# Moving a query projection and a pair of score rounds in the prologue of a two-cache decode kernel

## Chip, cores, metric

One core of one Trainium2 chip. The metric is device microseconds (us) of one execution; each quoted time is the median of the runs named with it. In the profile the engines are called PE (TensorE), DVE (VectorE), ACT (ScalarE), POOL (GpSimd) and SP (SyncE).

## The reference, cut to what matters

Two single-token attention blocks, A and B, with 32 query heads of 128 each. A reads all 32,768 keys and values of 32 heads (the large cache, 268 MB each). B reads the last 4,096 keys and values of 8 heads, each serving four query heads (the small cache, 8 MB each).

```python
q = (x @ wq).reshape(B, Sq, H, Dh)                  # query projection
scores = einsum("bhqd,bhkd->bhqk", q, k) * Dh**-0.5
p = softmax(scores)
o = einsum("bhqk,bhkd->bhqd", p, v)
out = o.reshape(B, Sq, H * Dh) @ wo                 # then A and B side by side
```

## The kernel before

All large loads are 4 MiB and go through one DMA queue (issued by SP) in program order. There are four big buffers: two for keys, two for values. The value buffers first hold the two query weights: B's in `v[0]`, A's in `v[1]`. A "unit" is one key buffer: TensorE (PE) transposes it in 16 batches of eight, VectorE (DVE) copies each batch out, and PE multiplies by the queries, one "pair" of steps behind. A "round" then takes the maximum, exponentiates, transposes the probabilities (`psPT`) and multiplies them with the values (`PV`). A "gather" is a small matmul at the end of a round. B has two rounds of one unit each, in the prologue; A has 32 rounds of two units, in a loop on PE.

```python
self.load_wq("B")                      # -> v[0]
for g in range(2):
    self.load_kv("k", "B", g, 0, 0)    # -> k[0], k[1]
self.load_wq("A")                      # -> v[1]
self.emit_qproj("B")
for g in range(2):
    self.emit_unit("B", g, 0, 0)       # transposes and scores of k[g]
    self.emit_round_end("B", g, 0)     # maximum, exponential, psPT
    if g == 0:
        self.emit_qproj("A")           # reads v[1]
    self.load_kv("v", "B", g, 0, 0)    # -> v[g], when its query weight has been read
    self.emit_PV("B", g, 0, 0)
    self.emit_gather("B", g, 0)
self.emit_spread("B")
# then the loop over A: per round, loads k[0], k[1], units, round end, loads v[0], v[1], PVs, gather
```

In this kernel each instruction raises at most one semaphore (a counter on which another engine waits), for one listener. If PE's instruction already has a listener (`to="dve"`), the message for SP is carried by PE's *next* instruction without one:

```python
# in emit_qproj: DVE is the listener, so SP must wait for a later PE instruction
o = self.op("pe", mm, (self.xsem[name], 16), self.landed("v", slot), self.accread, to="dve")
self.free["v"][slot] = o
# in assign()
if to is None:
    to = next((c for c in users + pending), None)
pending = [c for c in dict.fromkeys(pending + users) if c != to]
```

The units' transposes, `PV` and the second half of a gather all have a listener. The first score operation of a pair and the first half of a gather have none, so they carry SP's messages.

## Time and profile before

| | before |
|---|---|
| time, 3 runs | 1341.73 us (1341.38 to 1341.76) |
| profiled span | 1340.3 us |
| read from memory | 570.43 MB, mean 426 GB/s |
| PE / DVE / ACT busy | 71% / 59% / 5% |

From the page of the kernel before: the mean busy share of the 16 DMA engines (in tenths) and the GB/s they moved, in 40 equal slices of 33.5 us, and the main queue (packets, MB, share of the engines' span).

```profile
DMA  9799999999999999999999999999999999999998
GB/s 397 303 437 428 433 428 434 431 432 432 427 436 428 434 432 428 435 429 434 429 432 433 430 434 429 433 432 429 435 429 432 433 429 433 431 432 430 431 434 353
...
q1 hardware_dynamic: 21700, 570.44, 99.1%
```

Between the first slice and the last, the stream is full but for the second slice: at 303 GB/s, about 10 us of loading are missing there, (432 - 303)/432 of 33.5 us. From 140 to 1300 us the trace has a mean of 432 GB/s at a DMA share of 1.00, and no slice has more than 437. That a load could not go faster is not shown; with the DMA engines busy throughout, I took it that what a change to the prologue can win is a hole in this stream.

The stretches around it (window in us and its length; busy time of PE, PE's weight loads, DVE, ACT and POOL; granted TensorE clock; DMA share; GB/s):

```profile
51.00:52.00 1.00, 0.00 (x0) 0.00 (x0) 0.00 (x0) 0.00 (x0) 0.00 (x0) 0.50 0.91 377
52.00:53.00 1.00, 0.00 (x0) 0.00 (x0) 0.00 (x0) 0.00 (x0) 0.00 (x0) 0.50 0.22 90
53.00:54.00 1.00, 0.00 (x0) 0.00 (x0) 0.00 (x0) 0.00 (x0) 0.00 (x0) 0.50 0.06 25
54.00:60.00 6.00, 4.36 (x38) 1.37 (x39) 1.40 (x4) 0.00 (x0) 0.00 (x0) 0.50 0.00 0
60.00:61.00 1.00, 1.00 (x11) 1.00 (x12) 0.02 (x1) 0.00 (x0) 0.00 (x0) 0.50 0.65 98
61.00:62.00 1.00, 1.00 (x12) 1.00 (x10) 0.84 (x2) 0.00 (x0) 0.00 (x0) 0.50 0.54 213
62.00:63.00 1.00, 1.00 (x13) 1.00 (x11) 0.84 (x2) 0.00 (x0) 0.00 (x0) 0.50 1.00 410
```

DMA all but stops at 52.3 us and is back at full rate at 62. What SP and PE do meanwhile, from the timeline (start, length, engine, line; in brackets, idle time before it and what ended that):

```profile
30.70 29.20 SPq L291 DMA_DIRECT2D vbuf<-in_B_v_cache_dram  x2
...
44.24 3.55 PE L422 MATMUL psACC<-x_A,vbuf 128*128 128x1 bf16 x128 [2.58 <-DMA vbuf<-in_A_wq_dram]
...
54.03 3.59 PE L553 MATMUL psACC<-vbuf,ptsb 128*16 128x512 bf16 x32 [6.23 <-DMA vbuf<-in_B_v_cache_dram]
...
59.23 0.74 PE L596 MATMUL psG<-oc_B,hsel_B 128*32 128x1 f32 x4 [1.61 <-DVE oc_B L582]
...
59.94 10.77 SPq L291 DMA_DIRECT2D kbuf<-in_A_k_cache_dram  x2
```

A merged line with `x2` runs from the start of its first issue to the end of its last: the first of B's value loads was issued at 30.70, the second ended its issue at 59.90. It goes into the buffer that the second query projection had finished reading at 47.8, but SP heard of it from the gather at 59.23. The two key loads of A stand behind it. The DMA queue's own waits up to 140 us (total us, times, longest) say the same: one wait of 28.4 us ended by a gather.

```profile
SPq L291 <- PE psS L486: 65.1, 5, 21.6
SPq L291 <- PE psG L596: 57.0, 3, 28.4
```

### The profile page before, as it was taken

How to read it: one execution, taken by the hardware profiler on the slowest of the kernel's cores; microseconds unless marked ns; L12 is line 12 of the kernel's file. 1: busy time of each engine (PE TensorE's matmuls, PEld its weight loads, DVE VectorE, ACT ScalarE, POOL GpSimd, SP SyncE). 2: the span in 40 equal slices, each digit the busy share in tenths (PEclk: the TensorE clock that was granted, in tenths of full speed). 3: DMA queues.
4: the chain of work that ended last, by engine and by line, in shares of the span. 5: the costliest groups of instructions: out<-in, count | busy, mean ns of one | idle time of the engine just before them, and what ended most of it. 6: DMA issues, size and time to landing. Idle time of an engine off the chain costs nothing.

```text
span 1340.3 us, 41412 instructions
## 1 busy us (share of the span) xinstructions
PE 958.2 (71%) x19416; PEld 773.7 (58%) x19416; DVE 791.7 (59%) x1662; ACT 61.2 (5%) x201; POOL 2.0 (0%) x15
## 2 busy tenths in 40 slices
PE   3577767777666777766777686666877766777776
PEld 3455656566555665655556565555656655565663
DVE  3365656665555666555566665555676555566652
ACT  0000000000000000000000000000000000000000
POOL 0000000000000000000000000000000000000000
PEclk9677888898788889887888888788889787888888
DMA  9799999999999999999999999999999999999998
GB/s 397 303 437 428 433 428 434 431 432 432 427 436 428 434 432 428 435 429 434 429 432 433 430 434 429 433 432 429 435 429 432 433 429 433 431 432 430 431 434 353
DMA packets 22003, 570.64 MB, mean 426 GB/s; under 512 B 2530, under 2 KB 2532, under 8 KB 2788
## 3 DMA queue, kind: packets, MB, share of 16 engines
q1 hardware_dynamic: 21700, 570.44, 99.1%
q8 instruction: 10, 0.16, 0.1%
q10 hardware_dynamic: 288, 0.00, 0.0%
q14 instruction: 5, 0.04, 0.0%
HBM read 570.43 MB, written 0.00 MB: 426 GB/s over the span
## 4 chain that ended last, share of the span: by engine, by line
DMA 64%; PE 26%; issue 0%; DVE 0%; SPq 0%
DMA kbuf<-in_A_k_cache_dram 62%; PE psT L463 22%; PE psS L486 4%; DMA kbuf<-in_A_wo_dram 2%; PE psPT L625 0%; DVE out_sb L629 0%; SPq L291 0%
## 5 line engine op out<-in xcount | busy, mean ns | idle before, releaser
L466 DVE COPY kt<-psT 128x1024 bf16<-128x1024 bf16 x1056 | 655.7, 684 | 211.1 <-PE psT L463 208.9
L463 PE MATMUL psT<-ident,kbuf 128*128 128x128 bf16 x8448 | 576.5, 234 | 135.7 <-DMA kbuf<-in_A_k_cache_dram 126.1
L463 PEld LDWEIGHTS psT<-ident,kbuf 128*128 128x128 bf16 x8448 | 537.1, 106 | 227.7 <-DMA kbuf<-in_A_k_cache_dram 134.0
L553 PE MATMUL psACC<-vbuf,ptsb 128*2 128x128 bf16 (+1 forms) x8256 | 190.5, 273 | 45.4 <-ACT ptsb L531 22.0
L553 PEld LDWEIGHTS psACC<-vbuf,ptsb 128*2 128x2 bf16 (+1 forms) x8256 | 170.5, 106 | 66.7 <-ACT ptsb L531 30.5
L486 PE MATMUL psS<-kt,qw 128*32 128x512 bf16 x2048 | 157.6, 385 | 15.2 <-DVE kt L466 15.2
L528 PE MATMUL psPT<-ident,psb 128*128 128x128 bf16 x136 | 20.7, 307 | 139.3 <-ACT psb L518 139.3
L582 DVE SCALAR_TENSOR_TENSOR oc_A<-psACC,hot_A,oc_A 128x128 f32<-128x128 f32 x48 | 16.9, 351 | 146.2 <-PE psACC L553 146.2
L528 PEld LDWEIGHTS psPT<-ident,psb 128*128 128x128 bf16 x136 | 11.7, 130 | 149.4 <-ACT psb L518 149.4
L518 ACT ACTIVATE psb<-psS,nb_A 128x512 bf16<-128x512 f32 x32 | 22.0, 687 | 1164.5 <-DVE nb_A L517 1164.5
L486 PEld LDWEIGHTS psS<-kt,qw 128*32 128x32 bf16 x2048 | 34.0, 95 | 57.7 <-DVE kt L466 31.0
L579 DVE TENSOR_SCALAR oc_A<-psACC,hot_A 128x128 f32<-128x128 f32 x16 | 5.6, 351 | 92.8 <-PE psACC L553 92.8
L504 DVE TENSOR_REDUCE tr_in<-psS 128x1 f32<-128x512 f32 x34 | 23.5, 692 | 17.3 <-PE psS L486 17.3
L596 PE MATMUL psG<-oc_A,hw 128*32 128x128 f32 (+1 forms) x128 | 14.1, 220 | 22.1 <-DVE oc_A L582 19.4
L507 DVE COPY m<-tr_a 1x16 f32<-1x16 f32 (+1 forms) x136 | 22.3, 164 | 2.6
L513 DVE COPY b_A<-mr_A 1x16 f32<-1x16 f32 x128 | 21.1, 165 | 2.4
L596 PEld LDWEIGHTS psG<-oc_A,hw 128*32 128x32 f32 x128 | 6.5, 109 | 27.3 <-issue 27.3
L531 ACT ACTIVATE ptsb<-psPT 128x512 bf16<-128x512 bf16 x34 | 20.3, 597 | 17.6 <-PE psPT L528 17.6
L565 DVE TENSOR_SCALAR oc_A<-oc_A,alpha_A 128x129 f32<-128x129 f32 x16 | 4.6, 289 | 16.5 <-ACT alpha_A L521 16.5
L422 PE MATMUL psACC<-x_B,vbuf 128*128 128x1 bf16 x128 | 3.6, 165 | 13.3 <-DMA vbuf<-in_B_wq_dram 13.3
L422 PEld LDWEIGHTS psACC<-x_B,vbuf 128*128 128x128 bf16 x128 | 3.5, 104 | 13.3 <-issue 13.3
L521 ACT ACTIVATE alpha_A<-cm_A,nb_A 128x1 f32<-128x1 f32 x32 | 9.0, 282 | 0.0
(71 smaller groups left out, 106.3 us busy)
## 6 DMA issues: line engine op xcount, KB each, us to landing
kbuf<-in_A_k_cache_dram SPq DMA_DIRECT2D x64, 4096.0 KB, 28.1
vbuf<-in_A_v_cache_dram SPq DMA_DIRECT2D x64, 4096.0 KB, 28.3
kbuf<-in_B_k_cache_dram SPq DMA_DIRECT2D x2, 4096.0 KB, 27.9
vbuf<-in_B_v_cache_dram SPq DMA_DIRECT2D x2, 4096.0 KB, 18.3
vbuf<-in_B_wq_dram SPq DMA_DIRECT2D x1, 4096.0 KB, 12.4
vbuf<-in_A_wq_dram SPq DMA_DIRECT2D x1, 4096.0 KB, 41.8
kbuf<-in_B_wo_dram SPq DMA_DIRECT2D x2, 2048.0 KB, 25.6
kbuf<-in_A_wo_dram SPq DMA_DIRECT2D x1, 1536.0 KB, 22.2
```

The costliest lines, as they stand in the source:

```text
L463: inst = e.transpose(T[:, 128 * k:128 * k + 128], src[:, DH * tile:DH * tile + DH], self.ident[:, :])
L466: self.copies.append(self.op("dve", lambda v: v.tensor_copy(KT[:, :], T[:, :]), o, to="pe"))
L486: inst = e.matmul(self.S[32 * c:32 * c + 32, :], lhsT=win, rhs=self.kt[(bb + c // 2) % NKT][:, 512 * (c % 2):512 * (c % 2) + 512], start=f ...
L504: o = dve(lambda v: v.reduce_max(tr["in"][:, 0:1], self.S[:, :], axis=AXX), self.sdone, self.k_pool)
L507: x = dve(lambda v, c=c: v.tensor_copy(m4[0:1, W * c:W * c + W], tr["a"][32 * c:32 * c + 1, 0:W]), o)
L513: x = dve(lambda v, c=c: v.tensor_copy(t["b"][32 * c:32 * c + 1, 0:W].rearrange("p (k h) -> p k h", k=KC), t["mr"][0:1, k, :].unsqueeze(1) ...
L518: self.sread = self.op("act", lambda s: s.activation(out=self.psb[:, :], in_=self.S[:, :], func=ACTF.Exp, bias=t["nb"][:, k:k + 1], scale= ...
L528: inst = e.transpose(PT[:, 128 * jj:128 * jj + 128], self.psb[:, 128 * jj:128 * jj + 128], self.ident[:, :])
L531: self.ptread = self.op("act", lambda s: s.activation(out=self.ptsb[:, :], in_=PT[:, 0:512], func=ACTF.Copy), self.psread, to="pe")
L553: inst = e.matmul(acc[32 * c:32 * c + HG, 0:w], lhsT=pt[:, col:col + HG], rhs=vv[:, :, 16 * kc + 4 * c + jj, :], start=(kc == 0 and jj == ...
L582: self.oop = dve(lambda v, src=src, hot=hot: v.scalar_tensor_tensor(out=oc, in0=src, scalar=hot, in1=oc, op0=ALU.mult, op1=ALU.add), pv, b ...
L596: self.gath = self.op("pe", lambda e, c=c, c2=c2: e.matmul(self.G[0:32, c0 + c:c0 + c2], lhsT=win, rhs=t["oc"][:, c:c2], start=False, stop ...
```

## The change

Its intent: take both of B's score rounds before any of B's values, and do A's query projection inside the second unit, so that the buffer is released earlier. The round's end is split in two for that: statistics (`emit_stats`) and probability transpose (`emit_PT`). No computing is added or removed; what is cut from the diff below is bookkeeping (the rescaling factor is kept per round).

```diff
         self.load_wq("A")
         self.emit_qproj("B")
+        self.emit_unit("B", 0, 0, 0)
+        self.emit_stats("B", 0, 0)
+        self.emit_PT("B", 0, 0)
+        self.emit_unit("B", 1, 0, 0, lambda: self.emit_qproj("A"))
+        self.emit_stats("B", 1, 0)
         for g in range(2):
-            self.emit_unit("B", g, 0, 0)
-            self.emit_round_end("B", g, 0)
-            if g == 0:
-                self.emit_qproj("A")
+            if g == 1:
+                self.emit_PT("B", g, 0)
             self.load_kv("v", "B", g, 0, 0)
             self.emit_PV("B", g, 0, 0)
             self.emit_gather("B", g, 0)
@@
-    def emit_unit(self, name, g, r, u):
+    def emit_unit(self, name, g, r, u, late=None):
         slot = u if name == "A" else g
         for pr in range(4):
             for st in (2 * pr, 2 * pr + 1):
                 for half in range(2):
                     self.emit_T(slot, st, half)
+            if pr == 3 and late:
+                late()
             self.pending.append((name, g, r, u, pr, self.nbatch - 4))
             if len(self.pending) > 1:
                 self.emit_S(self.pending.pop(0))
```

More of the change, by code (lines that the diff above doesn't have):

```diff
@@ L337, in plan @@
         self.gath = self.lop = self.qcopy = self.hcopy = None
+        self.alpha = {}
         self.constants()
@@ L362, in plan @@
                 self.emit_unit("A", g, r, u)
-            self.emit_round_end("A", g, r)
+            self.emit_stats("A", g, r)
+            self.emit_PT("A", g, r)
             for u in range(2):
@@ L493, in emit_S, with emit_stats @@
         self.sdone = o
-    def emit_round_end(self, name, g, r):
+    def emit_stats(self, name, g, r):
         self.emit_S(self.pending.pop(0))
@@ L520, in emit_round_end, with emit_PT @@
             accum_out=t["rs"][:, k:k + 1]), o, self.psread, to="pe")
-        self.alpha = self.op("act", lambda s: s.activation(
+        self.alpha[name, k] = self.op("act", lambda s: s.activation(
             out=t["alpha"][:, k:k + 1], in_=t["cm"][1 - k if r else k][:, 0:1], func=ACTF.Exp,
             bias=t["nb"][:, k:k + 1], scale=self.SCALE), o, to="dve")
+    def emit_PT(self, name, g, r):
+        d, t = self.X[name], self.c[name]
         PT = self.PT[:, :].bitcast(BF16)
@@ L535, in emit_round_end @@
             self.hcopy = self.op("act", lambda s: s.activation(
-                out=self.hw[:, :], in_=t["hsel"][:, 32 - HG * g:64 - HG * g], func=ACTF.Copy, scale=on),
+                out=self.hw[:, :], in_=t["hsel"][:, 32 - d["HG"] * g:64 - d["HG"] * g], func=ACTF.Copy, scale=on),
                 self.k_sel, to="pe")
@@ L565, in emit_PV @@
             first = dve(lambda v: v.tensor_scalar_mul(t["oc"][:, :], t["oc"][:, :], t["alpha"][:, k:k + 1]),
-                        self.alpha, self.oop, self.gath, to="dve")
+                        self.alpha[name, k], self.oop, self.gath, to="dve")
         def denominator():
             if r > 0:
-                return dve(lambda v: v.tensor_add(lcol, lcol, t["rs"][:, k:k + 1]), first, self.alpha, to="dve")
-            return dve(lambda v: v.tensor_copy(lcol, t["rs"][:, k:k + 1]), self.alpha, first, to="dve")
+                return dve(lambda v: v.tensor_add(lcol, lcol, t["rs"][:, k:k + 1]), first, self.alpha[name, k], to="dve")
+            return dve(lambda v: v.tensor_copy(lcol, t["rs"][:, k:k + 1]), self.alpha[name, k], first, to="dve")
         if d["units"] == 1:
```

## The prediction

> **What bounds the kernel.** DMA. The page's DMA row is full in nearly all of the 40 slices: 570.4 MB read at a mean of 426 GB/s, and 20 us windows from 60 to 1320 us show a DMA share of 0.98 to 1.02 at 416 to 439 GB/s. [...] PE is busy 71%, DVE 59%. Each 4 MiB load takes about 9.7 us at that rate. The only hole outside start and tail is in the third slice (303 GB/s): 1 us windows show the share at 0.22 in 52-53, 0.06 in 53-54, zero from 54 to 60, full again from about 61: some 8.3 us.
>
> **Why the hole.** The first five loads (both query weights, two small-cache key tiles, first value tile) end at about 52.3 us. The sixth, the second value tile, goes to the buffer of the second query weight, so it needs that query projection (PE 44.2 to 47.8). Its release is signalled only by PE's next operation without an assigned listener, the gather after the first values (59.23): the queue's waits name that gather, and the timeline shows the issue at about 59.5. The first large-cache loads stand behind it in queue order.
>
> **What the change does.** No computing is added or removed. After the first round's probabilities PE goes straight on with the second unit's transposes, then the query projection, then the scores, whose first operation now carries the release.
>
> Costs from the trace:
> - First probability transpose ends at 41.7, unchanged.
> - Second unit's transposes: from first to last 10.6 us in unit one (24.5 to 35.1), 10.0 in unit two (59.9 to 69.9). They start cold: TensorE clock 0.50 from 40 us. [...] End at about 52.2.
> - Query projection: 3.55 us cold; warm perhaps 2.0 to 2.3 (estimate from the value product, which took 3.58 cold and 1.96 to 2.30 warm). End 54.2 to 55.8.
> - First score operation to issue: 0.40 us (69.93 to about 70.33 before).
>
> So the sixth load is issued at 54.6 to 56.2 instead of 59.5: 3.3 to 4.9 us earlier. The next two large-key loads follow at once, as both key buffers are free by then. The next value load waits for the first values' gather, at about 62, and the one after for the second's, about 72, while three queued loads keep DMA busy until about 85: no new hole. All of the gain is on the critical path, because the loop is DMA bound and a shift of its start goes through to the end. The hole is halved, not closed: some 4 us stay.
>
> **Prediction.** 1341.7 - 4.1 = 1337.6 us, range 1335.5 to 1340.0. Faster by over 2%: 0.005; within 2%: 0.99; slower by over 2%: 0.005.
>
> **What would show it right.** Hole from about 52.3 to 56.5 us in 1 us windows; second value load released by a score operation, not a gather; second query projection at about 52 us; loop's DMA share still about 1.00; everything later about 4 us earlier. Wrong: a second hole before 110 us, or one that stays 8 us.
>
> **What would make it wrong.** The transposes run cold longer (later issue); a release signalled by another operation than I think; DMA resuming later than 1.1 us after issue; or the shift given back in the loop's first iterations.

Its sum: transposes to 52.2, projection to 54.2 to 55.8, issue at 54.6 to 56.2 instead of 59.5, so 3.3 to 4.9 us, 4.1 in the middle, and 1341.7 - 4.1 = 1337.6 us. "At that rate" means about 431 GB/s, the mean from 60 to 1320 us in the trace of the kernel before; the same trace has eight transposes in 0.85 us at a recorded clock of 0.50 (60 to 62 us).

## The result, and the profile after

| | before | after |
|---|---|---|
| time | 1341.74 us, 4 runs (1341.38 to 1342.23) | 1338.36 us, 4 runs (1336.93 to 1339.06) |
| ratio after / before | | 0.9973 (95% interval 0.9956 to 0.9990) |
| profiled span | 1340.3 us | 1335.2 us |

A ratio here is the mean time of one kernel's fast runs over that of the other's of the same rounds, so it is not quite the ratio of the medians. The change is small, 0.27%, and clear of the noise.

The same two rows of the page, for the changed kernel: the second slice went from 303 to 377 GB/s, and no other slice moved by more than 10 GB/s.

```profile
DMA  9999999999999999999999999999999999999998
GB/s 394 377 427 436 426 436 426 438 425 438 426 437 427 436 428 434 430 434 429 435 429 435 428 435 429 435 429 434 430 432 432 432 432 431 432 432 432 431 433 354
```

The same stretches for the changed kernel. The hole starts at the same time and ends some 5 us sooner.

```profile
51.00:52.00 1.00, 1.00 (x46) 1.00 (x43) 1.00 (x3) 0.00 (x0) 0.00 (x0) 1.00 0.83 344
52.00:53.00 1.00, 1.00 (x46) 1.00 (x43) 0.23 (x1) 0.00 (x0) 0.00 (x0) 1.00 0.32 123
53.00:54.00 1.00, 1.00 (x46) 1.00 (x43) 0.00 (x0) 0.00 (x0) 0.00 (x0) 1.00 0.08 33
54.00:55.00 1.00, 1.00 (x21) 0.52 (x21) 0.19 (x1) 0.00 (x0) 0.00 (x0) 0.76 0.00 0
55.00:56.00 1.00, 1.00 (x16) 0.40 (x12) 0.24 (x1) 0.00 (x0) 0.00 (x0) 0.50 0.56 66
56.00:57.00 1.00, 1.00 (x16) 0.39 (x12) 0.90 (x4) 0.00 (x0) 0.00 (x0) 0.50 0.56 213
57.00:58.00 1.00, 1.00 (x13) 0.31 (x8) 0.91 (x5) 0.00 (x0) 0.00 (x0) 0.53 1.04 442
```

The timeline of the changed kernel, second unit to first gather:

```profile
40.71 5.45 PE L470 MATMUL psT<-ident,kbuf 128*128 128x128 bf16 x64
...
50.87 3.34 PE L427 MATMUL psACC<-x_A,vbuf 128*128 128x1 bf16 x128
...
54.14 1.57 PE L493 MATMUL psS<-kt,qz 128*32 128x512 bf16 x16
...
54.59 0.37 SPq L291 DMA_DIRECT2D vbuf<-in_B_v_cache_dram  x1
...
55.00 0.98 SPq L291 DMA_DIRECT2D kbuf<-in_A_k_cache_dram  x2
...
60.59 0.47 PE L606 MATMUL psG<-oc_B,hsel_B 128*32 128x1 f32 x4 [1.99 <-DVE oc_B L592]
```

PE starts the second unit's transposes at 40.71, with no wait for values; the projection follows at 50.87; the score operation at 54.14 tells SP, which issues the second value load at 54.59 and both key loads of A right behind it. In the queue's waits, time moved from the gathers to the score operations:

```profile
SPq L291 <- PE psS L493: 90.0, 6, 24.4
SPq L291 <- PE psG L606: 36.0, 3, 18.7
```

The profiled run was the fastest of its four, so 5.1 us of difference between the spans is more than the 3.4 us between the medians. The spread itself is taken up below.

### The profile page after: what moved, and what is told of

It is laid out like the page before. It is cut to its first block, busy times and chain, and to the rows that moved or that the text cites. A ratio compares the mean times of both kernels' runs of the same rounds, so it can differ in the third digit from the quotient of the medians.

```text
span 1335.2 us, 41413 instructions
## 1 busy us (share of the span) xinstructions
PE 954.6 (71%) x19416; PEld 771.0 (58%) x19416; DVE 791.1 (59%) x1662; ACT 61.1 (5%) x201; POOL 2.0 (0%) x15
## 4 chain that ended last, share of the span: by engine, by line
DMA 64%; PE 26%; issue 0%; DVE 0%; SPq 0%
DMA kbuf<-in_A_k_cache_dram 63%; PE psT L470 22%; PE psS L493 4%; DMA kbuf<-in_A_wo_dram 2%; PE psPT L635 0%; DVE out_sb L639 0%; SPq L291 0%
## 5 line engine op out<-in xcount | busy, mean ns | idle before, releaser
L563 PEld LDWEIGHTS psACC<-vbuf,ptsb 128*2 128x2 bf16 (+1 forms) x8256 | 169.0, 106 | 67.1 <-ACT ptsb L541 30.5
L538 PEld LDWEIGHTS psPT<-ident,psb 128*128 128x128 bf16 x136 | 11.6, 130 | 145.0 <-ACT psb L525 144.8
```

Of the source, the lines that this page charges most:

```text
L538: inst = e.transpose(PT[:, 128 * jj:128 * jj + 128], self.psb[:, 128 * jj:128 * jj + 128], self.ident[:, :])
L563: inst = e.matmul(acc[32 * c:32 * c + HG, 0:w], lhsT=pt[:, col:col + HG], rhs=vv[:, :, 16 * kc + 4 * c + jj, :], start=(kc == 0 and jj == ...
```

## The experiments

Every kernel gave a correct result. "Hole" below is the loading that is missing: the sum over 1 us windows of (432 - GB/s)/432, once for 50 to 65 us and once for 115 to 135 us. (It counts the slow ramp at 60 to 62 us as well, so it gives 9.3 us for the kernel before, where the prediction read 8.3 from the shares.) "Issue" is when SP issues B's second value load.

| kernel | issue | hole at 50-65 | hole at 115-135 | span of the profiled run | median, 5 runs (lowest, highest) | ratio to before |
|---|---|---|---|---|---|---|
| before | 59.5 | 9.3 | 0.2 | 1340.3 | 1342.18, 9 runs (1341.85, 1342.51) | 1 |
| after, again | 55.2 | 4.9 | 0 | 1335.7 | 1339.01 (1337.44, 1339.18) | 0.9976 |
| e1 signal only | 48.2 | 0 | 4.7 | 1336.8 | 1339.57 (1338.51, 1340.18) | 0.9981 |
| e2 key load first | 59.5 | 0.2 | 4.0 | 1335.7 | 1337.58 (1337.48, 1338.93) | 0.9969 |
| e4 late release | 61.5 | 11.1 | 0.5 | 1342.1 | 1343.86 (1343.70, 1345.86) | 1.0019 |
| e3 projection early | 50.9 | 0.3 | 0 | 1332.3 | 1335.53 (1334.07, 1336.62) | 0.9952 |
| e5 projection first | 54.5 | 4.1 | 0.5 | 1335.0 | 1336.62 (1335.88, 1337.06) | 0.9958 |
| e6 key load first, on changed | 55.3 | 0.2 | 1.9 | 1333.3 | 1335.59 (1335.01, 1336.90) | 0.9954 |
| e7 two signals | 48.1 | 0 | 0 | 1332.6 | 1334.74 (1334.30, 1335.34) | 0.9946 |
| e8 early with signal | 49.0 | 0 | 0 | 1332.8 | 1334.57 (1334.22, 1334.68) | 0.9943 |
| e9 early and loop signal | 47.9 | 0 | 0 | 1332.6 | 1334.32 (1334.20, 1334.78) | 0.9942 |
| after, third time | 57.0 | 6.8 | 0.2 | 1337.7 | 1338.36 (1337.45, 1339.45) | 0.9971 |

The runs of before are those of the first batch; in the other two batches its median was 1342.18 and 1342.16. The three batches ran on three different chips; each ratio is to the kernel before in the same batch. Issue, hole and span of before are those of its profile above.

### e1: the release alone, in the old order

Theory A was that the time is the hole, and the hole is the late release of one buffer. Rival B was that the gain comes from PE's order of work, which lets PE reach the loop earlier.

```diff
                 self.emit_qproj("A")
+                self.op("pe", lambda e: e.transpose(
+                    self.T[0][:, :].bitcast(BF16)[:, 0:128], self.ident[:, :], self.ident[:, :]))
```

> The kernel before, with its order of work kept; one small transpose into an idle PSUM bank follows the second query projection and carries the release of its buffer to the DMA queue. Theory A (the time is the hole in the DMA stream, and the hole is the late release of that buffer): the second value load is issued at about 48 us instead of 59.5, the hole of about 8.3 us closes, and the kernel takes about 1333.5 us, less than the changed kernel. Theory B (the gain comes from the order of PE's work, which lets the loop start earlier): nothing in PE's order has moved, so about 1341.7 us.

The first part came true: SP heard from the small transpose, issue was at 48.2 us, and the hole was gone. But the time was 1339.57, not 1333.5. Windows of this kernel (same columns) show where the gain went:

```profile
52.00:61.00 9.00, 5.09 (x59) 2.43 (x59) 1.99 (x5) 0.00 (x0) 0.00 (x0) 0.70 1.01 422
121.00:125.00 4.00, 0.98 (x5) 0.37 (x5) 0.35 (x1) 0.00 (x0) 0.00 (x0) 0.66 0.03 8
```

A new hole of some 4 us had opened at 121 us. SP's issues around it:

```profile
31.31 17.23 SPq L291 DMA_DIRECT2D vbuf<-in_B_v_cache_dram  x2
...
95.03 10.08 SPq L291 DMA_DIRECT2D kbuf<-in_A_k_cache_dram  x2
124.14 0.80 SPq L291 DMA_DIRECT2D vbuf<-in_A_v_cache_dram  x2
```

The last loads before it are the two keys at 95.03 to 105.11; the next is the first value load of the loop's second round, at 124.14, told by the gather of the first round (123.87). Closing the first hole moved the stream forward by 8 us or so, but PE's chain to that gather did not move, and it had only some 5 us to spare: in the kernel before the seven loads after the hole would have lasted from 61 to about 129 us (7 times 9.7), and the gather came at 123.6. Part of e1's chain are two stalls of PE, 1.51 and 3.95 us, that no wait in the trace explains (see the last section). Without them the gather would have come at about 118.4 us (an estimate: 123.87 less both), before DMA ran dry at about 121. No run takes the stalls away, so how much of the second hole is theirs stays open. Theory A alone had fallen, and so had B alone, since time was won without a change of order.

### e2: queue order alone

```diff
             self.load_kv("v", "B", g, 0, 0)
+            if g == 0:
+                self.load_kv("k", "A", 0, 0, 0)
@@
-                self.load_kv("k", "A", g, r, u)
+                if i > 0 or u > 0:
+                    self.load_kv("k", "A", g, r, u)
```

> The kernel before, with PE's order and every release kept; only the first large-cache key load goes into the DMA queue ahead of the second small-cache value load instead of behind it. Theory A: it is issued at about 35.5 us and follows the fifth load without a gap, while the value load is still issued at about 59.5, so the hole closes and the time is about 1333.5 us. Theory B: about 1341.7 us.

The key load filled the first hole though the value load was issued as late as before (59.5 us, with a hole of 0.2 us and not 9.3), which shows that it was the head of the queue that blocked. The time was 1337.58, again 4 us short of the expectation, with the same new hole at 121 us (4.0 us).

### e4: the changed order with the old release

The comment is added here, and a second part of the edit, which keeps that operation in `gath0`, is cut.

```diff
             if g == 1:
                 self.emit_PT("B", g, 0)
+                self.free["v"][1] = self.gath0   # the first gather's first half
```

> The changed kernel with PE's order kept, but the second value load is made to wait for the gather of the first values again, as in the kernel before. Theory A: the load is issued at about 60.9 us, some 1.3 us later than in the kernel before, and the time is about 1343 us; the whole gain is gone. Theory B: PE's order is that of the changed kernel, so about 1338 us.

Theory A was right here: 1343.86 us, slower than the kernel before. SP's issues:

```profile
30.61 31.23 SPq L291 DMA_DIRECT2D vbuf<-in_B_v_cache_dram  x2
61.88 0.98 SPq L291 DMA_DIRECT2D kbuf<-in_A_k_cache_dram  x2
```

The second value load's issue ended at 61.84, 1.9 us later than before, and the median is 1.7 us higher. So PE's order wins nothing by itself while the release is late. Together, e1 and e4 suggested a theory A2: there are two limits, the release of the weight's buffer and, behind it, PE's chain up to the first values of the loop. The change moves both.

### after again

> The changed kernel itself, on the same chip as the others. Both theories: about 1338.4 us, with a spread over its runs of about 2 us as in the first four; the second value load is issued at about 54.6 to 55.4 us and a hole of about 3.5 us stays in the DMA stream.

1339.01 us and a spread of 1.7 us, about as expected; the hole was 4.9 us and not 3.5.

### e3: the projection two pairs earlier

```diff
-            if pr == 3 and late:
+            if pr == 1 and late:
```

> The changed kernel with one number changed: the second query projection follows the second pair of steps of the second unit, not the fourth. The last batch showed that in the kernel before an early release alone only moves the hole: a new one of some 4 us opens at 121 us, as the first values of the loop are released at 124 us by a PE chain that starts late. Theory A2 (two limits: the release of the query weight's buffer, and the PE chain up to the first values of the loop; the change moves both): the second value load is issued at about 50 us, before the queue runs dry at 52, the first hole closes, the loop's first gather comes at about 113 us, well before the queue runs dry at about 121, and the time is about 1334.0 us (8.2 us below before). Theory A (one hole, one release): the same here. Rival C (some 4 us of any such gain are always lost to something not yet seen): about 1338 us, no better than the changed kernel.

Both holes were gone, and rival C was out: 1335.53 us, 3.5 us below the changed kernel in the batch before, though 1.5 above the expectation. The load was issued at 50.9 us, only 1.4 before the queue ran dry, and the runs spread over 2.6 us.

### e5: the projection in front of the unit

```diff
-        self.emit_unit("B", 1, 0, 0, lambda: self.emit_qproj("A"))
+        self.emit_qproj("A")
+        self.emit_unit("B", 1, 0, 0)
```

> The changed kernel with the second query projection taken out of the second unit and put right before it, so only the order of scores ahead of values is left of the change. PE then waits for that weight, which lands at about 44 us, and the release comes with the first score operation after the projection and 64 transposes. Theory A2: issue at about 53.4 us, against about 55 in the changed kernel, a hole of some 2 us, and about 1.2 us less than the changed kernel: some 1337.3 us, so the place within the unit is not what wins. Theory D (the place within the unit is what wins, since PE no longer waits for the weight): slower than the changed kernel by the wait of 2.6 us, about 1341 us.

1336.62 us: theory D fell, and the place *within* the unit is not what the change wins by. The issue came at 54.5 us (53.4 expected), so the hole was 4.1 us and not 2. PE did wait 2.5 us for the weight, and it cost nothing, since the release came no later.

### e6: queue order, on the changed kernel

The edit is that of e2, made to the changed kernel.

> The changed kernel with the first large-cache key load ahead of the second small-cache value load in the DMA queue, the same edit that took the kernel before to about 1337.6 us with a new hole at 121 us. Theory A2: the first hole closes; the second values now land only at about 73 us, PE waits for them, the loop's first transposes start at about 78 us and its first gather comes at about 118 us, just before the queue runs dry at about 121, so no second hole, or one below 1 us: about 1334.5 us. Theory A: 1334. Rival C: 1338.

1335.59 us, 2.0 below e2. The second hole shrank from 4.0 to 1.9 us, not to under 1: PE had to wait until 73.95 us for B's second values, which now stood behind a key load, so the loop's first transposes began at 81.9 and not at 78, and its first gather at 120.9. I had allowed 5 us from those values to the loop; the second product, gather and spread took 8. The second limit works as A2 says, with less slack than I had counted.

### e7: two signals, no change of order

e1, and in the loop:

```diff
                 self.emit_PV("A", g, r, u)
+                if u == 0:
+                    self.op("pe", lambda e: e.transpose(
+                        self.T[0][:, :].bitcast(BF16)[:, 0:128], self.ident[:, :], self.ident[:, :]))
```

> The kernel before with the early release of the first of these experiments, and a second small transpose in the loop, after the first value product of each round, which carries the release of that value buffer instead of the gather after the second product. PE's order of work is that of the kernel before. Theory A2: the loop's first value buffer is released at about 117 us instead of 124, the second hole closes as well, and the time is about 1334 us, though PE reaches the loop as late as before. Theory B (PE must reach the loop earlier): the hole at 121 us stays and the time is about 1339.5 us.

1334.74 us, 7.4 us below before and well below the changed kernel, with PE's order of work untouched. The windows in which e1 had its hole:

```profile
52.00:61.00 9.00, 5.20 (x58) 2.42 (x59) 1.96 (x5) 0.00 (x0) 0.00 (x0) 0.69 1.01 421
121.00:125.00 4.00, 0.98 (x6) 0.37 (x6) 0.35 (x1) 0.00 (x0) 0.00 (x0) 0.69 1.00 426
```

PE is as busy from 121 to 125 us as in e1, 0.98 us, and stalls as long just before its last two matmuls (3.96 us), but DMA moved 426 GB/s there and not 8: SP issued the first of the loop's value loads at 116.93 us and not at 124.14. So it was not PE's late arrival as such, but the gather that carried the message for a buffer that had been read some 7 us earlier. That is the clearest of these runs: both holes closed when nothing was changed but who says that a buffer is free, and when.

### e8, e9 and the spread of the changed kernel

The kernel before spread over 0.7 us in nine runs, the changed one over about 2 us. In e8 the projection comes after the first pair, followed by a small transpose that carries the release, so that nothing is close to a limit. e9 adds e7's loop signal.

```diff
-        self.emit_unit("B", 1, 0, 0, lambda: self.emit_qproj("A"))
+        self.emit_unit("B", 1, 0, 0, lambda: self.emit_qproj("A") or self.signal())
@@
-            if pr == 3 and late:
+            if pr == 0 and late:
@@
+    def signal(self):
+        self.op("pe", lambda e: e.transpose(
+            self.PT[:, :].bitcast(BF16)[:, 512:640], self.ident[:, :], self.ident[:, :]), self.ptread)
```

> The changed kernel with the second query projection after the first pair of steps of the second unit, and a small transpose right behind it that carries the release. The earlier run that closed the first hole with the changed order issued its load at 50.9 us, only 1.4 us before the queue runs dry, and its runs spread over 2.6 us. Theory E (kernels whose hole is ended by an instruction behind clock-dependent transposes spread; one with slack everywhere doesn't): issue at about 48.2 us, no hole, about 1334.3 us and a spread of 1 us or less. Rival (the spread comes from elsewhere, say from the last projections): about 1335.5 us with a spread of 2 us or more.

> The run before in this batch with the early release of the loop's first value buffer as well. Theory A2: with no hole left after the start, a further early release is worth nothing: the same within 0.5 us, about 1334.3 us. If it is faster by 1 us or more, some hole in the loop is still open.

> The changed kernel again, on the same chip as these two, for a direct comparison: about 1338.8 us, spread about 2 us, and a hole of about 3.5 to 4 us in its profile. The two above should be about 4.5 us below it.

e8 took 1334.57 us with a spread of 0.46 us, e9 1334.32, the changed kernel beside them 1338.36 with a spread of 2.0. (Its profile, of its slowest run, has a hole of 6.8 us where 3.5 to 4 were expected.) Windows of e8 in both places:

```profile
52.00:61.00 9.00, 8.52 (x132) 5.02 (x129) 7.30 (x16) 0.00 (x0) 0.00 (x0) 0.92 1.01 421
121.00:125.00 4.00, 4.00 (x73) 3.22 (x70) 4.00 (x8) 0.00 (x0) 0.00 (x0) 1.00 1.03 442
```

The third profile of the changed kernel happened to be of a slow run (1339.45 us), the first of a fast one (1336.93), so the two can be laid side by side. PE up to the operation that tells SP, first the fast run of the changed kernel, then the slow one:

```profile
24.39 5.08 PE L470 MATMUL psT<-ident,kbuf 128*128 128x128 bf16 x64 [7.59 <-DMA kbuf<-in_B_k_cache_dram]
...
40.71 5.45 PE L470 MATMUL psT<-ident,kbuf 128*128 128x128 bf16 x64
...
50.87 3.34 PE L427 MATMUL psACC<-x_A,vbuf 128*128 128x1 bf16 x128
54.14 1.57 PE L493 MATMUL psS<-kt,qz 128*32 128x512 bf16 x16
```

```profile
24.53 6.60 PE L470 MATMUL psT<-ident,kbuf 128*128 128x128 bf16 x64 [7.83 <-DMA kbuf<-in_B_k_cache_dram]
...
42.27 6.30 PE L470 MATMUL psT<-ident,kbuf 128*128 128x128 bf16 x64
...
53.28 3.34 PE L427 MATMUL psACC<-x_A,vbuf 128*128 128x1 bf16 x128
56.55 1.05 PE L493 MATMUL psS<-kt,qz 128*32 128x512 bf16 x16
```

The first unit's 64 transposes took 5.08 us in the one and 6.60 in the other, the second unit's 5.45 and 6.30: 2.37 us together. The issue was 2.39 us later (54.59 and 56.98), the span 2.5 us longer. The second profile of the changed kernel lies between the two (5.29 and 5.58 us, issue at 55.2, span 1335.7). The transposes start at a slower pace, eight in 0.85 us (12 or 13 of them in a 1 us window), and reach their full pace, 32 in 1.96 us, at different times. In the second unit the recorded clock goes from 0.50 to 1.00 at about 44.3 us in the fast run and 47.6 in the slow one, 3.6 and 5.3 us after the unit's first transpose. In the first unit the clock column reads 1.00 throughout, and only the pace shows the change, at about 27 and 30.5 us. So the change of pace came at different distances from the start of the work; what sets the distance is not shown. In the kernel before, the end of the hole depends on a load that landed at 54.0 and not on the transposes, so it does not spread; and e8, which has slack, does not either. The tie between clock and spread rests on these three profiles and on e8; why e5's runs lie below the changed kernel's, with like profiles (1335.0 and 1335.2), was not tried. One reason is at hand: in e5 only one of the two stretches of transposes counts, because the landing of the weight at 44.4 hides the other.

## Why the prediction was right, point by point

- **What bounds the kernel.** Right. All thirteen profiles have 431 to 432 GB/s from 140 to 1300 us, and the span follows the sum of the holes to within 2.6 us, over a range of 11.6. (From kernels with the old hole to those without any, 9.5 counted us of hole gave 7.6 us of span. Most of the rest is lost at the end: the page's last slice has 353 GB/s in the kernel before and 339, 332 and 337 in e7, e8 and e9, which is 1.1 to 1.6 us of loading.)
- **Why the hole.** Right, and shown by three independent edits: an earlier message (e1), another load at the head of the queue (e2), and the old message put back (e4).
- **Issue between 54.6 and 56.2 us.** Measured 54.6, 55.2 and 57.0 in three profiles, the last outside the range. The terms: the second transposes gave way to the projection at 50.9 in the first profile (predicted 52.2), 51.5 and 53.3 in the others; the projection took 3.34 us in all three. So in the first two profiles an early warm-up made good a projection that was longer than hoped, and that is luck. The hope of 2.0 to 2.3 us for a warm projection was wrong. It was taken from a product with 128 columns moving per matmul, while here one column moves, and 3.34 us over 128 is 26.1 ns each. The projection hardly gained from the clock: 27.7 ns each at a recorded clock of 0.50 (3.55 us, in the kernel before), 26.1 at 1.00. (Each of these matmuls also loads its own weights, and the weight loads keep the same pace, 3.31 us for 128; no run here tells which of the two sets the pace.)
- **The whole gain goes through to the end.** Right for this change: no second hole, and 5.1 us of span for 4.9 us of earlier issue in the first profile. The reason given, a DMA-bound loop, was not enough: e1 and e2 have the same loop, and each lost some 4 us again at 121 us. The prediction followed the loads only to 85 us. That the change also moved the loop's first gather, from 123.57 to 117.35 us, was not worked out in it as a condition, so this point was in part luck.
- **1337.6 us.** Measured 1338.36; 1339.01 and 1338.36 in later batches, all inside the range of 1335.5 to 1340.0. The gain was 3.2 to 3.8 us by medians and not 4.1. The mis-sized term is probably the projection: 3.34 us, where the middle of the predicted 2.0 to 3.55 is 2.8; the transposes' end scattered around the predicted 52.2 (50.9, 51.5, 53.3).
- **What it did not see.** That the old order had only some 5 us of slack at the loop's first values. The prediction did not count this place for either kernel, and so theory A expected 1333.5 of e1 and e2. A gain of 8 us was never there for the early release alone.

## What to carry to other kernels

When a DMA-bound kernel has a hole in its stream, ask first which instruction *tells* the queue that the buffer is free, and not only which one frees it: here the two were 11 us apart, and one tiny instruction that carries the message (twice) won 7.4 us, twice as much as the changed order of work (3.2 to 3.8). After closing a hole, look for the next place where the stream has little slack, because the gain can stop there (in e1 and e2 some 4 us of it were lost again at 121 us); and if a kernel's runs spread more than before, look whether its limit now sits behind work whose pace changes with the clock (here the second unit's 64 transposes took 5.45 us in a fast run, with the clock at 1.00 from about 44.3, and 6.30 in a slow one, from about 47.6).

The fastest kernels here are e8 and e9: 1334.57 and 1334.32 us, against 1338.36 for the changed kernel in the same batch and 1342.16 for the kernel before.

## What else the traces show

- In e1, PE stood still for 1.51 and 3.95 us in the loop's first pass, with no wait that the trace can name, just ahead of single last matmuls:

```profile
116.43 0.22 PE L555 MATMUL psACC<-vbuf,ptsb 128*2 128x128 bf16 x1 [1.51 <-issue]
117.09 1.96 PE L555 MATMUL psACC<-vbuf,ptsb 128*2 128x128 bf16 x127 [0.44 <-DVE oc_A L581]
123.00 0.26 PE L555 MATMUL psACC<-vbuf,ptsb 128*2 128x128 bf16 x1 [3.95 <-issue]
123.87 0.72 PE L598 MATMUL psG<-oc_A,hw 128*32 128x1 f32 x4 [0.61 <-DVE oc_A L584]
```

  In the changed kernel it was 5.46 us ahead of the first gather, and 0.62 or 0.63 us, ended by DVE, in rounds two to nine:

```profile
109.93 1.96 PE L563 MATMUL psACC<-vbuf,ptsb 128*2 128x128 bf16 x128 [1.21 <-DVE oc_A L589]
117.35 0.71 PE L606 MATMUL psG<-oc_A,hw 128*32 128x1 f32 x4 [5.46 <-issue]
```

  In the kernel before it was 2.74 us there. One packet of 0.02 MB on the instruction queue was moved between 118 and 128 us in e1 (the longer stall is from 119.05 to 123.00) and one between 114 and 115 us in the changed kernel, within the stall. What causes the stalls is not shown. In e1 they are part of the chain that opened e1's second hole.
- Full clock came while PE ran nothing but transposes (the profile lists them as matmuls with the identity): in the changed kernel PE runs nothing else from 40.3 us to 46.1, after 4.2 us of idle time, and the recorded clock goes from 0.50 to 1.00 at about 44.3. 32 transposes take 1.96 us after that (at 46.63 and 49.07), where eight had been taking 0.85.
- The time to full pace varied: the first unit's 64 transposes, after an idle time of 7.6 to 7.8 us, took 5.08, 5.29 and 6.60 us in the three profiles of the changed kernel and 5.82 in the kernel before. By the pace in 1 us windows, full speed came some 3 us after the first of them in the fast run of the changed kernel and some 6 in the slow one (an estimate). Two such stretches made up 2.37 of the 2.5 us between these two runs.
- The point is what it costs when the message that a buffer is free rides on a later instruction: 11.4 us from the end of the projection (47.79) to the gather that told SP (59.23), in the kernel before.
